# Longformer attention and MLP mixer on one core: global rows by one-hot matmuls, an MLP head tile by tile, transposes moved over the period edge, one normalisation per query tile, first casts on ScalarE

## The chip, the cores and the metric

The kernel runs on one core of one Trainium2 chip. The metric is the device time of one execution in microseconds (us). A timed comparison runs both kernels in the same rounds on the same chip.

Names: PE is TensorE (PEld its weight loads), DVE VectorE, ACT ScalarE, POOL GpSimd, SP SyncE.

## The reference

Eight batches, eight heads, 576 positions, head size 64. Attention has a band of 32 positions to each side and eight global positions, which see all and are seen by all. The result is laid out as 576 x 512 and goes through a mixer: an MLP over tokens with a residual, and an MLP over channels with a residual.

```python
scores = scale * np.matmul(q, k.transpose(0, 1, 3, 2))
mask = np.abs(pos[:, None] - pos[None, :]) <= 32
mask = mask | is_global[:, None] | is_global[None, :]
attn = softmax(np.where(mask, scores, -1e9))          # shortened
x = (attn @ v).transpose(0, 2, 1, 3).reshape(B, S, H * D)
h = np.maximum(xt @ w_tok1, 0.0) @ w_tok2             # xt: x with tokens last
u = x + h.transpose(0, 2, 1)
out = u + np.maximum(u @ w_ch1, 0.0) @ w_ch2
```

## The kernel before

The work is arranged in periods. In period b the channel MLP of batch b (`dense`: tiles `b1p_*` of M4, then `op_*` of M5) is merged on PE with the attention and the token MLP of batch b+1 (`sparse`). Batch 0 has no partner for its attention, so a preamble of 58 us comes first, in which PE mostly waits. The parts that the change and the argument touch:

```python
def gather_t(t):                     # global rows of four batches, fetched by indirect DMA on POOL
    pg = psv([P, 2, P], F16, name=f"pg_{t}")
    for ti in range(2):
        nc.vector.tensor_copy(out=g16[ti][t], in_=g32[ti][t])
        nc.tensor.transpose(out=pg[:, ti, :], in_=g16[ti][t], identity=ident)
    ...
def norm(b, tau, hf, sh, ps):        # twice per query tile, once per half of the heads
    nc.vector.reciprocal(out=rr[r], in_=pq[r, :, D])
    nc.vector.tensor_tensor(out=x16s[b % 2][...], in0=pq[r, :, 0:D], in1=rr[r]..., op=ALU.mult)

def M1(b, ch):                       # token MLP, first layer
    ...
    nc.scalar.activation(out=a1, in_=ps, func=AF.Relu)        # 128 x 1024

def M2(b, part):                     # second layer and residual, two token tiles at a time
    ...
    nc.vector.tensor_add(out=s["u16"][:, 2*part : 2*part+2], in0=x16[:, 2*part : 2*part+2], in1=ps)

def M3(b, part):                     # transpose of u: by PE for batch 0, by DMA for the others
    if part < 2 and b == 0:
        ...
    elif part < 2:
        for i in range(2):
            tau = 2 * part + i
            nc.sync.dma_start_transpose(out=s["uT"][:, :, P*tau : P*tau+P], in_=s["u16"][:, tau, :])

def sparse(b):                       # (weight, work); merge() spreads it over the dense work of b-1
    u = [(8.0 if b == 1 else 0.5, lambda: globals_(b))]
    u += [t(0), t(1), sa(0), sb(0), t(2), sm(0), sa(1), sb(1), t(3), ...]
    ...
    u += [(1.3, lambda: (M2(b, 0), M3(b, 0))), (1.3, lambda: (M2(b, 1), M3(b, 1)))]
    u += [(6.0, lambda: (M2(b, 2), M3(b, 2) if b % 2 else None))]

def cast0(p):                        # batch 0: f32 to f16, q on ACT, k on DVE
    cast_qk(0, slice(2*p, 2*p + 2), (nc.scalar.copy, nc.vector.tensor_copy))

cast0(0); T(0, 0); TE(0, 0); masks_a(); cast0(1); gather_t(0); globals_(0)
T(0, 1); TE(0, 1); S_(0, 0, 0); masks_b(); cast0(2); ...
```

`T` is ten PE transposes of a pair of heads, `TE` their four copies out of PSUM by DVE. `S_` is scores and exp, `SM` the two masked products per pair of heads on DVE (`e_all`). POOL clears `e_all` with one large memset early in the preamble. In the tile names `pv` is the attention output, `a1p` and `hp` are the two layers of the token MLP, `u` is x plus their result (`ul` its last rows), `uT` the transpose of `u`, `b1p` and `op` are the two layers of the channel MLP and `osb` the output. The first channel matmul of batch b+1, `b1p_0`, needs the four DMA transposes `uT` of that batch.

The softmax here doesn't subtract the row's maximum and nothing guards it: scores larger than these inputs give would overflow.

## Time and profile before

| | before |
|---|---|
| median of 4 runs, in the rounds shared with the changed kernel | 376.06 us (374.57 to 377.19) |
| span of the profiled run, mean clock | 375.8 us, 0.979 |
| first PV matmul (end of the wait for attention of batch 0) | 40.06 us |
| end of the token MLP's first layer (`a1p`) | 49.58 us |
| first channel matmul `b1p_0` of batch 0 | 58.45 us |

From the page of the kernel before: span, busy time by engine, two rows of the 40 slices (each digit the busy share of a slice in tenths; PEclk the granted clock), and the chain of work that ended last, by engine.

```profile
span 375.8 us, 6776 instructions
...
PE 319.2 (85%) x2713; PEld 168.2 (45%) x2713; DVE 202.4 (54%) x507; ACT 136.6 (36%) x269; POOL 117.3 (31%) x167
...
PE   0145868988699998999699989997999989997994
...
PEclk9999989999899999999899999999899999999998
...
PE 71%; DVE 12%; ACT 6%; DMA 6%; SPq 3%; issue 2%; DVEq 0%; ACTq 0%
```

PE is busy for 85% of the span and carries 71% of the last chain. The first six digits of its row are where it is not yet busy.

The stage table of the kernel before, cut at the three moments of the small table. Columns: the stretch, its length, busy time of each engine with the number of instructions, granted clock, DMA share, GB/s.

```profile
...
core 0: us, PE busy (x) PEld busy (x) DVE busy (x) ACT busy (x) POOL busy (x), PEclk, DMA share, GB/s
0.00:40.06 40.06, 12.38 (x115) 7.50 (x116) 29.93 (x87) 12.71 (x27) 28.00 (x61) 1.00 0.91 194
40.06:49.58 9.52, 8.99 (x92) 5.86 (x92) 5.82 (x20) 0.00 (x1) 7.07 (x9) 1.00 0.96 192
49.58:58.45 8.87, 4.82 (x26) 2.24 (x26) 3.87 (x5) 1.02 (x1) 7.72 (x11) 0.81 1.05 175
58.45:375.80 317.35, 293.05 (x2480) 152.61 (x2479) 162.80 (x396) 122.90 (x241) 74.51 (x89) 0.98 0.68 78
```

In the first 40.06 us DVE is busy for 29.93, PE for 12.38: the preamble is bound by DVE and what it waits for. In the last row PE is busy for 293.05 of 317.35 us. The 1.00 of the first stretch says nothing: the clock record of this profile begins only at 46.09 us, and what lies before a record is printed as 1.00.

The chain of waits of the kernel before around 17 us (start, length, what), and the timeline of POOL at that time (start, length, engine, line, operation, tiles):

```profile
...
17.21 2.26 DVE g_k_170 L324
```

```profile
...
17.12 2.26 POOL L254 MEMSET e_all<- 128x2560 f16 x1
```

The cast of the gathered rows is a 128x128 piece of work; it took 2.26 us exactly while the POOL memset of 2.26 us ran.

The waits of PE in the kernel before, for the first channel matmul of each period: who waited, at which line, for whom, us in total, times, longest.

```profile
...
PE b1p_0_2209 L571 <- DMA uT_2150<-u_3_2136: 2.8, 1, 2.8
PE b1p_0_3240 L571 <- DMA uT_3181<-u_5_3167: 2.7, 1, 2.7
PE b1p_0_1178 L571 <- DMA uT_1111<-u_1_1104: 2.6, 1, 2.6
PE b1p_0_4240 L571 <- DMA uT_4197<-u_7_4183: 2.5, 1, 2.5
PE b1p_0_2760 L571 <- DMA uT_2695<-u_4_2678: 1.4, 1, 1.4
```

At these edges PE waits for the DMA transposes of the next batch, or, into batch 2, for DVE (the last `osb`). With the two that are cut (1.3 us into batch 6 and 1.2 into batch 2) it is 14.5 us in all.

### The profile page before, as it was taken

The page shows a single profiled execution, that of the slowest core. Times are in us where ns is not written, and L with a number is a line of the kernel's source. Part 1 is how long each engine was busy: PE and PEld are TensorE (multiplying, and loading weights), DVE is VectorE, ACT ScalarE, POOL GpSimd, SP SyncE. Part 2 cuts the span into 40 slices and gives each one's busy share as a digit, 9 for nine tenths or more (in the row PEclk, how much of TensorE's full clock was granted, in tenths as well). Part 3 has the DMA queues.
Part 4 walks back from the last instruction along what each step waited for, and adds up shares of the span by engine and source line. Part 5 has one row for each costly group of instructions (what it writes and reads, how often), then busy time and mean ns, then how long its engine had stood idle before and what let it go on. Part 6 is the DMA issues. An engine that isn't in the chain of part 4 may idle for free.

```text
span 375.8 us, 6776 instructions
## 1 busy us (share of the span) xinstructions
PE 319.2 (85%) x2713; PEld 168.2 (45%) x2713; DVE 202.4 (54%) x507; ACT 136.6 (36%) x269; POOL 117.3 (31%) x167
## 2 busy tenths in 40 slices
PE   0145868988699998999699989997999989997994
PEld 0022524454255644464346535453547444553541
DVE  3888644875347562765246554764366546753021
ACT  2036014921078014911196007801492119411610
POOL 7992589962008300750035300930000000000000
PEclk9999989999899999999899999999899999999998
DMA  5959999998509953996339841994200140015012
GB/s 150 252 94 240 261 164 119 130 141 74 127 2 120 81 103 84 67 126 81 105 20 118 103 96 53 113 99 90 72 2 29 57 113 0 2 58 127 2 56 84
DMA packets 127487, 35.81 MB, mean 95 GB/s; under 512 B 114656, under 2 KB 122720, under 8 KB 127456
## 3 DMA queue, kind: packets, MB, share of 16 engines
q0 software_dynamic: 88768, 14.65, 51.4%
q1 hardware_dynamic: 38400, 20.72, 20.5%
q8 instruction: 21, 0.34, 0.4%
q14 instruction: 10, 0.08, 0.1%
q10 hardware_dynamic: 288, 0.01, 0.0%
HBM read 36.12 MB, written 9.44 MB: 121 GB/s over the span
## 4 chain that ended last, share of the span: by engine, by line
PE 71%; DVE 12%; ACT 6%; DMA 6%; SPq 3%; issue 2%; DVEq 0%; ACTq 0%
SPq L560 3%; DMA lq<-in_q_dram 1%; DVE e_all L434 1%; ACT e_all L415 1%; ACT e_all L424 1%; DMA uT_1111<-u_1_1104 1%; ACT e_all L422 1%; ACT e_all L423 1%; PE op_4_4431 L597 1%; PE op_3_3737 L597 1%; PE op_4_1695 L597 1%; PE op_3_2706 L597 1%; PE op_3_4415 L597 1%; PE op_2_4399 L597 1%; PE op_1_4383 L597 1%
## 5 line engine op out<-in xcount | busy, mean ns | idle before, releaser
L571 PEld LDWEIGHTS <-wc_180 128*128 128x128 f16 x384 | 32.8, 99 | 55.1 <-issue 22.4
L434 DVE TENSOR_TENSOR e_all<-e_all,bandm 128x1040 f16<-128x1040 f16 x64 | 41.9, 696 | 1.2
L340 POOL DMA_DIRECT2D qn_83<-in_q_dram x15 | 13.5, 898 | 46.1 <-PE pT_3_1297 L370 23.4
L484 PEld LDWEIGHTS <-e_all 128*128 128x128 f16 x320 | 25.0, 100 | 5.8 <-issue 2.3
L340 POOL DMA_DIRECT2D qn_84<-in_q_dram x15 | 13.2, 879 | 40.8 <-PE pT_3_2873 L370 20.1
L489 PEld LDWEIGHTS <-e_all 128*128 128x128 f16 x256 | 19.0, 101 | 1.3
L345 POOL DMA_DIRECT2D vsh_87<-in_v_dram x15 | 12.8, 895 | 16.6 <-PE pv_1_1_1516 L489 2.5
L345 POOL DMA_DIRECT2D vsh_88<-in_v_dram x15 | 12.6, 839 | 16.0 <-PE pv_1_1_982 L489 1.5
L340 POOL DMA_DIRECT2D kn_85<-in_k_dram x15 | 13.6, 907 | 0.0
L532 PEld LDWEIGHTS <-w_179 128*128 128x128 f16 x80 | 7.9, 100 | 12.2 <-issue 4.3
L340 POOL DMA_DIRECT2D kn_86<-in_k_dram x15 | 13.3, 888 | 0.0
L428 DVE TENSOR_TENSOR eg<-e_all,bandm 128x160 f16<-128x160 f16 x32 | 7.5, 236 | 10.6 <-ACT e_all L424 10.6
L370 PEld LDWEIGHTS <-qn_83 128*128 128x128 f16 x80 | 7.1, 119 | 13.6 <-ACT qn_83 L352 9.2
L404 PEld LDWEIGHTS <-kT_125 64*128 64x128 f16 x160 | 6.2, 101 | 13.8 <-issue 13.0
L584 PEld LDWEIGHTS <-wc_180 128*128 128x128 f16 x192 | 10.9, 98 | 0.6
L601 DVE TENSOR_TENSOR osb_0_4380<-u_7_4183,op_0_4367 128x512 f32<-128x512 f16 x1 | 0.7, 686 | 17.7 <-PE op_0_4367 L597 17.7
L404 PEld LDWEIGHTS <-kT_126 64*128 64x128 f16 x160 | 5.2, 94 | 10.1 <-issue 3.8
L370 PEld LDWEIGHTS <-kn_85 128*128 128x128 f16 x80 | 6.8, 120 | 4.8 <-DVE kn_85 L352 4.4
L370 PE MATMUL pT_0_215<-ident,qn_83 128*128 128x128 f16 x5 | 0.7, 309 | 8.7 <-ACT qn_83 L352 8.7
L512 PEld LDWEIGHTS <-w_177 128*128 128x128 f16 x64 | 5.6, 99 | 5.0
L370 PEld LDWEIGHTS <-qn_84 128*128 128x128 f16 x80 | 5.7, 98 | 3.5
L597 PEld LDWEIGHTS <-b_7_4239 128*128 128x128 f16 x48 | 4.7, 98 | 5.4
(1308 smaller groups left out, 845.4 us busy)
## 6 DMA issues: line engine op xcount, KB each, us to landing
lv<-in_v_dram SPq DMA_DIRECT2D x6, 256.0 KB, 8.4
wc_180<-in_moe_w_ch_dram POOLq DMA_DIRECT2D x3, 512.0 KB, 7.1
wc_181<-in_moe_w_ch_dram POOLq DMA_DIRECT2D x3, 512.0 KB, 7.7
qn_83<-in_q_dram POOLq DMA_DIRECT2D x12, 128.0 KB, 4.3
kn_85<-in_k_dram POOLq DMA_DIRECT2D x12, 128.0 KB, 4.4
qn_84<-in_q_dram POOLq DMA_DIRECT2D x12, 128.0 KB, 4.2
kn_86<-in_k_dram POOLq DMA_DIRECT2D x12, 128.0 KB, 4.3
vsh_87<-in_v_dram POOLq DMA_DIRECT2D x9, 128.0 KB, 4.2
```

What stands on the lines that cost most here:

```text
L340: nc.gpsimd.dma_start(out=dst[b % 2][0:n, t], in_=ten[b, :, P * t : P * t + n, :].rearrange("h p d -> p h d"))
L345: nc.gpsimd.dma_start(out=vsh[b % 2][r0:r1, c, :, 0:D], in_=v[b, :, j0 : j0 + (r1 - r0), :].rearrange("h p d -> p h d"),)
L370: nc.tensor.transpose(out=pT[:, ti, P * t : P * t + P], in_=n[b % 2][:, t, 2 * p : 2 * p + 2, :], identity=ident)
L404: nc.tensor.matmul(ps[:, par, off : off + n], lhsT=kT[r, P * c : P * c + P], rhs=qf[r, lo : lo + n], start=True, stop=True,)
L434: nc.vector.tensor_mul(out=eh, in0=eh, in1=bandm)
L484: nc.tensor.matmul(o, lhsT=e_all[:, h, tau, EW - P - sh : EW - sh], rhs=vsh[b % 2][:, tau, h, :], start=False, stop=last and tau == NT - 1,)
L489: nc.tensor.matmul(o, lhsT=e_all[:, h, tau + 1, 0:P], rhs=vsh[b % 2][:, tau + 1, h, :], start=False, stop=last)
L532: nc.tensor.matmul(ps[:, i, :], lhsT=w2[:, ch, P * tau - sh : P * tau - sh + P], rhs=s["a1"][:, ch, :], start=(ch == 0), stop=(ch == 1),)
L560: nc.sync.dma_start_transpose(out=s["uT"][:, :, P * tau : P * tau + P], in_=s["u16"][:, tau, :])
L571: nc.tensor.matmul(ps, lhsT=wc1[:, cc, P * j : P * j + P], rhs=s["uT"][:, cc, :], start=(cc == 0), stop=(cc == 3))
L584: nc.tensor.matmul(ps[:, i, :], lhsT=wc1[:, cc, P * j : P * j + P], rhs=s["uTl"][:, cc, :], start=(cc == 0), stop=(cc == 3),)
L597: nc.tensor.matmul(ps, lhsT=w, rhs=wc2[:, j, :], start=(j == 0), stop=(j == NJ - 1))
```

## The change

The intent: shorten the DVE work ahead of the first PV, shorten the head of the first batch's MLP, and fill the waits at the period edges. Its core, cut:

```diff
+    def G0(p):      # batch 0: global rows as one-hot matmuls on PE (N = 8), no gather
+        for ti, n in enumerate((qn, kn)):
+            for t in range(NT):
+                nc.tensor.matmul(pg[:, p, ti, :], lhsT=n[0][:, t, 2*p : 2*p+2, :], rhs=ohq[:, t, :], ...)
...
     def cast0(p):
-        cast_qk(0, ..., (nc.scalar.copy, nc.vector.tensor_copy))
+        cast_qk(0, ..., (nc.scalar.copy, nc.scalar.copy))
...   # masks_b: nine narrow scalar_tensor_tensor -> four wide products; mf: DVE -> POOL
-        nc.vector.tensor_scalar(out=mf, in0=it_f, ...)
+        nc.gpsimd.tensor_scalar(out=mf, in0=it_f, ...)
...   # the large memset of e_all moves behind masks_c; gather(0) moves to the end of the preamble
-    nc.gpsimd.memset(e_all[:, :, :, 0:64], 0.0)
+    masks_c()
+    nc.gpsimd.memset(e_all[:, :, :, 0:64], 0.0)
...   # PV: one two-bank PSUM tile (psV bufs 2 -> 1), one reciprocal and one product per query tile
-        for hf in range(2):
-            norm(b, tau, hf, sh, pss_[hf])
+        nc.vector.reciprocal(out=rr[r], in_=pq[r, :, :, D])
+        nc.vector.tensor_tensor(out=x16s[b % 2][r, tau, :]..., in0=pq[r, :, :, 0:D], in1=rr[r]..., op=ALU.mult)
...   # head of batch 0: relu in two halves, residual and transposes tile by tile, copies on ACT
+        if b == 0:
+            nc.scalar.activation(out=a1[:, 0], in_=ps[:, 0], func=AF.Relu)
+            nc.vector.tensor_scalar(out=a1[:, 1], in0=ps[:, 1], scalar1=0.0, scalar2=None, op0=ALU.max)
-    for part in range(3):
-        M2(0, part)
-        if part < 2:
-            M3(0, part)
+    M23_first(0); M23_first(1); M3_first(0); M23_first(2); M3_first(1)
+    M23_first(3); M3_first(2); M3_first(3); M2(0, 2)
...   # edges: globals and the first two transposes of batch b+1 go to the end of sparse(b)
-        u = [(8.0 if b == 1 else 0.5, lambda: globals_(b))]
-        u += [t(0), t(1), sa(0), ...]
+        if b < 3:
+            u += [(8.0 if b == 1 else 0.5, lambda: globals_(b)), t(0), t(1)]
...
-        u += [(6.0, lambda: (M2(b, 2), M3(b, 2) if b % 2 else None))]
+        u += [(3.0, lambda: (M2(b, 2), M3(b, 2) if b % 2 else None))]
+        if 3 <= b + 1 < B:
+            n = b + 1
+            u += [(0.5, lambda: globals_(n)), (1.5, lambda: (T(n, 0), TE(n, 0))), (0.5, lambda: (T(n, 1), TE(n, 1)))]
+        else:
+            u += [(2.0, lambda: None)]
```

The loads of batch b+2 are split and issued from inside `sparse(b)` (q and k after the last transposes that read the old tiles, v after the last PV). In the preamble `load_wt()` and `pads(0)` also change place, and the copy `it_f` that `mf` reads goes to POOL with it.

## The prediction

> **What bounds it now.** The page gives PE 85% of the span, DVE 54%; the chain that ended last is 71% PE. From about 58 us on, matmuls run almost back to back, and what is lost sits at the edges between batches. Until then (a first-batch preamble of 58.45 us, to the first channel matmul b1p_0) PE is busy for only 26 us; the chain of waits there runs mostly through DVE: g_k cast 2.26 us (held up while POOL's 2.26 us memset runs), masks, four 1.5 us transpose evictions, k casts squeezed between them.
>
> **Preamble, three parts (chain and timelines of before).**
> 1. To the first PV matmul, 40.1 us. Removed from DVE: 8 k casts (about 4.5 us with their slow ones), gather casts and copies (about 3.5 us), nine narrow mask products (3.1 us to four wider, est. 1.7), mf (1.1 us, goes to POOL). POOL loses four gathers (5.2 us). Added: 40 matmuls with N=8, est. 1 us per pair, in PE idle time. All casts on ACT delay the first transposes by about 0.5 us. Following DVE through the new order, with the two score PSUM buffers, I get the first PV at 33.5 to 35.5, so 5.5 us saved.
> 2. PV and first token matmul: 40.1 to 49.6. Normalisation per tile instead of per half: two times 0.2+0.43 becomes est. 0.95 us, alternating PSUM: about 1 us saved.
> 3. MLP head: 49.6 to 58.45. Relu 1.03 us split over two engines, adds 1.22 us halved (0.69) and overlapped, uT copies to ACT: est. 6.4 instead of 8.9 us.  2.4 us saved.
>
> Sum 9 us, all on the critical path.
>
> **Period edges.** Waits list: b1p_0 waits for the DMA transposes 2.6, 1.2, 2.8, 1.4, 2.7, 1.3, 2.5 us. Landing follows the first hp group by 7.7 us: add 1, four serial issues of 1.3 on the SP queue, 2.5 landing. After three of these waits the next 20 to 30 matmuls run slow (b1p_0 1.50 to 1.87 us instead of 0.86), costing about 1.8 us each[...]. The change puts 1.1 us of transposes and 0.3 us of scores into five of seven edges (into batches 2 to 6): 1.5 us each at the two long ones, 0.55 at the three short (there hp_1 moves later), and the two slow-clock episodes should mostly go (3 us). Edge 0 to 1: same slot, but hp_1 comes 1.3 us earlier: 1.3 saved. Edge 6 to 7: nothing fills it, hp_1 comes later: 1.3 lost, perhaps 1.7 more by clock. PV now has one two-bank buffer: norm 1.0 us against 1.29 us of interposed matmuls, hidden mostly; M4 stage fuller for ACT (14 of 17 us busy): 1 us lost. Net 5 us.
>
> **Prediction.** 376.5 − 9 − 5 = 362.5 us; 8 in 10: 357 to 368. Faster by over 2%: 0.93; within 2%: 0.06; slower: 0.01.
>
> **What would show it.** First b1p_0 near 49.5; first PV near 34.5; b1p_0 waits of about 1 us or less into batches 2 to 6, longer than 3 into 7; no long stall of pv on norm.
>
> **What would make it wrong.** POOL's memsets and casts blocking DVE f16 products; weight loads, now issued earlier, delaying q/k landings; ACT saturating in M4; PE colder in the sparser head; single PV buffer stalls.

The 1 us per pair for the one-hot matmuls names no source and is the author's estimate; the trace of after has the ten of the second pair within 0.45 us (13.85 to 14.30).

## More of the kernel before

A difference of one or two microseconds between two medians can be clock alone.

## The result

The changed kernel took 361.89 us in the median of 4 runs (361.25 to 363.89), against 376.06 us. The ratio is 0.9635, with a 95% interval from 0.9583 to 0.9687. Ratios here and below are the mean time of one kernel's runs over that of the other's of the same rounds, so not quite the ratio of the medians quoted.

The page of the changed kernel, the same lines as before:

```profile
span 359.5 us, 6784 instructions
...
PE 316.5 (88%) x2753; PEld 167.6 (47%) x2753; DVE 186.2 (52%) x420; ACT 140.8 (39%) x281; POOL 121.8 (34%) x171
...
PE   0466789896999999898999989898999999996994
...
PEclk9999999999899999999999999999999999998999
...
PE 71%; DVE 13%; ACT 6%; DMA 4%; issue 2%; SPq 2%; another core or an unknown queue 0%; DVEq 0%
```

The stage table of the changed kernel, cut at its first PV, the end of `a1p` and its first `b1p_0`; columns as in the table of before:

```profile
...
0.00:32.55 32.55, 12.70 (x154) 8.94 (x155) 22.05 (x74) 15.75 (x35) 27.73 (x53) 1.00 1.02 218
32.55:41.37 8.82, 8.39 (x92) 5.80 (x92) 4.45 (x10) 0.00 (x0) 8.61 (x16) 1.00 1.22 212
41.37:48.30 6.93, 4.25 (x28) 1.78 (x28) 4.27 (x8) 2.94 (x5) 6.62 (x11) 1.00 1.16 190
48.30:359.50 311.20, 291.21 (x2482) 151.10 (x2481) 155.47 (x328) 122.07 (x241) 78.89 (x94) 0.99 0.72 82
```

The three preamble stretches are 7.5, 0.7 and 1.9 us shorter (40.06 to 32.55, 9.52 to 8.82, 8.87 to 6.93), and the periods 6.15 us (317.35 to 311.20). In the first stretch DVE lost 7.9 us of work (29.93 to 22.05) and PV came 7.5 us earlier, so the stretch shrank nearly one for one with DVE. These differences come to 16.3 us, and the medians differ by 14.2: the profiled execution of before took 377.74 us, more than any of its four timed runs, and that of after was the fastest of its four.

The waits of PE at the edges of the changed kernel:

```profile
...
PE b1p_0_4137 L594 <- DMA uT_4094<-u_7_4071: 3.2, 1, 3.2
PE b1p_0_1195 L594 <- DMA uT_1152<-u_1_1131: 2.6, 1, 2.6
PE b1p_0_2751 L594 <- DMA uT_2667<-u_4_2638: 1.2, 1, 1.2
```

They belong to batches 7, 1 and 4. Two more are cut, 0.7 us into batch 5 and 0.6 into batch 3; into 2 and 6 there is no wait left. Taking the time from each `b1p_0` to the next, the periods changed as follows (positive: shorter).

| period, from the `b1p_0` of batch | 0 | 1 | 2 | 3 | 4 | 5 | 6 | 7, to the end |
|---|---|---|---|---|---|---|---|---|
| before, us | 42.54 | 43.13 | 38.10 | 43.41 | 37.92 | 43.33 | 37.78 | 31.14 |
| after, us | 41.18 | 43.06 | 37.05 | 41.68 | 37.15 | 40.41 | 37.94 | 32.73 |
| shorter by | 1.36 | 0.07 | 1.05 | 1.73 | 0.77 | 2.92 | -0.16 | -1.59 |

The last value is a clock drop. The timeline of PE in the changed kernel at the edge into batch 7 (the second number of a row is the time that a group of matmuls took, x4 the number in it, the bracket the idle time before):

```profile
...
326.77 1.02 PE L594 MATMUL b1p_0_4137<-uT_4094,wc_181 128*128 128x512 f16 x4 [3.20 <-DMA uT_4094<-u_7_4071]
327.63 1.65 PE L594 MATMUL b1p_1_4143<-uT_4094,wc_181 128*128 128x512 f16 x4
329.07 1.91 PE L594 MATMUL b1p_2_4149<-uT_4094,wc_181 128*128 128x512 f16 x4
330.78 1.29 PE L594 MATMUL b1p_3_4155<-uT_4094,wc_181 128*128 128x512 f16 x4
```

Four 128x512 matmuls took 1.03 us in each of the eight rows that follow (`b1p_4` to `b1p_11`, cut). Here three groups took 1.65, 1.91 and 1.29 us after an idle of 3.20 us.

### The profile page after: what moved, and what is told of

It is laid out like the page before. It is cut to its first block, busy times and chain, and to the rows that moved or that the text cites. A ratio compares the mean times of both kernels' runs of the same rounds, so it can differ in the third digit from the quotient of the medians.

```text
span 359.5 us, 6784 instructions
## 1 busy us (share of the span) xinstructions
PE 316.5 (88%) x2753; PEld 167.6 (47%) x2753; DVE 186.2 (52%) x420; ACT 140.8 (39%) x281; POOL 121.8 (34%) x171
## 4 chain that ended last, share of the span: by engine, by line
PE 71%; DVE 13%; ACT 6%; DMA 4%; issue 2%; SPq 2%; another core or an unknown queue 0%; DVEq 0%
DVE e_all L452 3%; ACT e_all L433 2%; DMA lq<-in_q_dram 1%; SPq L583 1%; ACT e_all L442 1%; ACT e_all L441 1%; DMA uT_2667<-u_4_2638 1%; PE op_4_4328 L620 1%; PE op_3_2168 L620 1%; PE op_3_1163 L620 1%; PE op_3_4312 L620 1%; PE op_2_4296 L620 1%; PE op_1_4280 L620 1%; PE op_0_4264 L620 1%; PE op_2_4081 L620 1%
## 5 line engine op out<-in xcount | busy, mean ns | idle before, releaser
L594 PEld LDWEIGHTS <-wc_181 128*128 128x128 f16 x384 | 32.8, 99 | 47.3 <-issue 17.2
L505 PEld LDWEIGHTS <-e_all 128*128 128x128 f16 x256 | 19.1, 101 | 1.3
L344 POOL DMA_DIRECT2D vsh_88<-in_v_dram x15 | 12.7, 879 | 13.9 <-PE pv_0_1964 L505 1.7
L388 PEld LDWEIGHTS <-qn_83 128*128 128x128 f16 x80 | 6.3, 110 | 11.6 <-ACT qn_83 L351 8.5
L607 PEld LDWEIGHTS <-wc_181 128*128 128x128 f16 x192 | 11.1, 98 | 0.8
L548 PEld LDWEIGHTS <-w_180 128*128 128x128 f16 x72 | 7.0, 98 | 8.4
L524 PEld LDWEIGHTS <-w_178 128*128 128x128 f16 x64 | 5.6, 99 | 4.9 <-issue 0.2
L388 PEld LDWEIGHTS <-qn_84 128*128 128x128 f16 x80 | 5.7, 98 | 3.8 <-issue 0.7
L620 PEld LDWEIGHTS <-b_7_4136 128*128 128x128 f16 x48 | 4.7, 98 | 5.4
L620 PEld LDWEIGHTS <-b_6_3726 128*128 128x128 f16 x48 | 4.6, 98 | 5.2
```

What stands on the lines that cost most here:

```text
L344: nc.gpsimd.dma_start(out=vsh[b % 2][r0:r1, c, :, 0:D], in_=v[b, :, j0 : j0 + (r1 - r0), :].rearrange("h p d -> p h d"),)
L388: nc.tensor.transpose(out=pT[:, ti, P * t : P * t + P], in_=n[b % 2][:, t, 2 * p : 2 * p + 2, :], identity=ident)
L505: nc.tensor.matmul(o, lhsT=e_all[:, h, tau + 1, 0:P], rhs=vsh[b % 2][:, tau + 1, h, :], start=False, stop=last)
L594: nc.tensor.matmul(ps, lhsT=wc1[:, cc, P * j : P * j + P], rhs=s["uT"][:, cc, :], start=(cc == 0), stop=(cc == 3))
L607: nc.tensor.matmul(ps[:, i, :], lhsT=wc1[:, cc, P * j : P * j + P], rhs=s["uTl"][:, cc, :], start=(cc == 0), stop=(cc == 3),)
L620: nc.tensor.matmul(ps, lhsT=w, rhs=wc2[:, j, :], start=(j == 0), stop=(j == NJ - 1))
```

## The experiments

Twelve kernels ran, all timed in three rounds, all correct, each with one profile. "Before" means the kernel before in the same rounds; its medians were 375.59, 375.56, 377.34 and 375.56 us in the four groups of rounds.

### edges_only: the kernel before with only the new `sparse` schedule and its loads

```diff
-    def sparse(b):  # of before
+    def sparse(b):  # of after, load_qk16 and load_v16 in it
```

> The kernel before with the new sparse schedule and its loads alone (transposes of batches 3 to 7 moved over the period edge, the loads with them); preamble, normalisation and PV buffers as before. Theory: filling the waits at the edges is worth what the two traces differ by after the first channel matmul, 16.3 - 10.0 = 6.3 us, whatever the preamble does: about 370 us (369 to 371), the five filled edges wait about 1.1 us or less, the edge into batch 7 waits over 3 us. Rival: the edge gain depends on the other parts (merged normalisation frees the vector engine there): then 373 or more, and new waits on the vector engine or on PV buffers show in the periods.

Measured: 368.80 us (368.19 to 370.78), ratio 0.9821 [0.9767, 0.9875], so faster, but not clear of 2%. From the first `b1p_0` to the end it took 310.5 us, against 317.35 in before and 311.20 in after. The whole gain of the periods comes from the schedule and is there without any preamble change. The wait into batch 7 was 3.20 us here too, but this time no slow stretch followed: the next 25 matmuls took 5.60 us.

This run also cleared up the head. It has the old head, but reached it with another history of the clock. The timelines of PE in the head (here the second number is the time of a group, x8 or x4 the matmuls in it), before first, then edges_only:

```profile
...
52.99 1.04 PE L550 MATMUL pu_0_611<-ident,u_0_602 128*128 128x128 f16 x8 [1.32 <-DVE u_0_602 L537]
53.82 1.91 PE L532 MATMUL hp_1_621<-a_0_600,w_179 128*128 128x512 f16 x4
```

```profile
...
52.12 0.62 PE L552 MATMUL pu<-ident,u 128*128 128x128 f16 x8 [1.31 <-DVE u L539]
52.58 1.03 PE L534 MATMUL hp<-a,w 128*128 128x512 f16 x4
```

The same eight transposes took 1.04 us in before and 0.62 here, the same four `hp_1` matmuls 1.91 and 1.03. The head of the kernel before had lost about 1.2 us to the clock (8.87 us from `a1p` to `b1p_0`, 7.66 here), behind two idle times of PE of 1.11 and 1.32 us.

### head_only: the kernel before with only the tile-by-tile head

```diff
-        nc.scalar.activation(out=a1, in_=ps, func=AF.Relu)
+        ...   # relu in two halves for batch 0
-    for part in range(3): M2(0, part); M3(0, part)
+    M23_first(0); M23_first(1); M3_first(0); ...
```

> The kernel before with the tile-by-tile MLP head of batch 0 alone (with the split relu and the transposed copies on the scalar engine). Theory: the head from the end of the first token matmul to the first channel matmul goes from 8.9 to about 7.1 us, as in the changed kernel, and the time to about 374.3 us. Rival: the head gains only beside the rest of the change (a warmer TensorE, a freer vector engine): then under 0.7 us of it shows, the time stays at 375.5 or more.

Measured: 375.63 us (372.43 to 376.70), ratio 0.9974 [0.9905, 1.0043]; by time alone inconclusive. In the profile the head takes 5.92 us, at a clock of 1.00. Against the 7.66 us of edges_only, also at 1.00, the tile-by-tile head is worth 1.7 us; against the profiled run of before it shows 2.9. The rest of that profile, after `b1p_0`, was 1.2 us longer than in before (318.56 and 317.35 us), and it hides the gain: after `b1p_0`, and before the drop at the very end, the clock was halved for 13.7 us in this profile and for 10.2 us in that of before. In after the head takes 6.93 us and not 5.92: there the casts and transposes of the late gather of batches 1 to 3 are issued on DVE and PE ahead of `b1p_0`. gather_clear, below, has the head of after without this late gather, and there it takes 5.91 us.

### gather_back: the changed kernel with the indirect gather for batch 0 again

```diff
+    gather(0)                       # early, as in before
-    G0(0); G0(1); G0(2); G0(3)
+    gather_t(0); globals_(0)
```

> The changed kernel with batch 0's global rows fetched by the indirect gather again (issued early on POOL, cast, transposed, copied), all else as changed; no one-hot matmuls. Theory: what the preamble gained is the shorter chain through the vector engine (k casts moved to the scalar engine, wider mask products, no cast held by a memset), not the one-hot rows: first PV matmul at 33 to 34.5 us instead of 32.6, time 362 to 364 us. Rival (the title of the change): the gather itself was the cost, so first PV goes back to 36 us or later and the time to 366 or more.

Measured: 368.81 us (367.23 to 371.16, 6 runs), ratio 0.9806 [0.9763, 0.9850], not clear of 2%. First PV at 39.58 us, 7.0 later than in after. By its limits (36 us or later, 366 us or more) the rival came true, but its reason did not, as gather_clear shows. The timeline of DVE in this run, the last pair of masked products (x2, one record), and of POOL at that time:

```profile
...
32.42 5.68 DVE L453 TENSOR_TENSOR e_all<-e_all,bandm 128x1040 f16<-128x1040 f16 x2
```

```profile
...
33.27 1.88 POOL L352 CAST qn<-lq 128x2048 f16<-128x2048 f32 x1
...
35.66 1.88 POOL L352 CAST kn<-lk 128x2048 f16<-128x2048 f32 x1
```

The same two products take 1.31 us, and 5.68 us when POOL casts q and k of batch 1 beside them. With the gather issued early, POOL gets to its casts for batch 1 at 33.27 us, while DVE, which is late, still has its last products to do; in after the casts start at 36.71 us, when the products have been done for 6 us. Why DVE is held is not shown. What the traces show is which DVE work took longer beside POOL work: products of two SBUF inputs (5.68 us against 1.31 here) and casts from SBUF (2.33 us beside the memset in before, 0.62 in memset_only, below). DVE copies from PSUM of 128x512 took 0.68 to 0.69 us with or without POOL work beside them.

### gather_clear: gather_back, with POOL's casts for batch 1 kept away

```diff
         load_wc1(h0)
+    gather(1)                       # in the slot where after issues gather(0): POOL is busy longer
     SM(0, 3)
...
-            gather(1)
```

> As gather_back (batch 0's global rows by the indirect gather), but the second gather of POOL is issued where the changed kernel issues its first, so that POOL's casts of batch 1 start some 5 us later and no longer run beside the last mask product of batch 0, which took 5.7 us instead of 1.3 in gather_back. Theory: of the 7 us that gather_back lost, 4.4 were that collision, and about 3 us are the gather's own cost on the vector engine: first PV matmul at 35 to 36 us (after: 32.6, gather_back: 39.6), time 364 to 365.5 us. Rival: the loss is the gather's own latency whatever POOL does: first PV stays at 38 us or later, time at 367.5 or more.

Measured: 364.12 us (363.76 to 367.31, 5 runs), ratio 0.9688 [0.9651, 0.9724]; first PV at 34.85 us. The last pair of products in the timeline of DVE:

```profile
...
32.47 1.31 DVE L453 TENSOR_TENSOR e_all<-e_all,bandm 128x1040 f16<-128x1040 f16 x2
```

So the 7.0 us of gather_back are two things: the gather itself, with what its early issue delays on POOL, 2.3 us (34.85 against 32.55), and an accident of order on POOL, 4.7 us (39.58 against 34.85). The one-hot matmuls are worth the first number, give or take: in seven profiles with the preamble of after the first PV lay between 31.91 and 32.60 us.

### memset_only: the kernel before with one memset moved behind the v casts

```diff
-    nc.gpsimd.memset(e_all[:, :, :, 0:64], 0.0)
     ...
     castv(0)
+    nc.gpsimd.memset(e_all[:, :, :, 0:64], 0.0)
```

> The kernel before with one POOL memset (the 128x2560 pads of e_all, 2.26 us) moved from before the v casts to after them, nothing else. Theory: the vector engine's cast of the gathered k rows (2.3 us) was only held by this memset, so it falls to about 0.3 us and the first PV matmul comes about 2 us earlier (38 us), time about 374.2. Rival: the hold only moves to another vector instruction that then runs beside the memset (mask products or k casts grow by 1 us or more), first PV stays within 0.7 us of 40.1, time 375.5 or more.

Measured: 376.57 us (376.40 to 376.72), ratio 1.0017 [0.9973, 1.0061]: nothing gained; first PV at 39.43 us, 0.6 earlier, as the rival said. The timeline of DVE in this run:

```profile
...
17.11 0.62 DVE L323 CAST g_k<-g_k 128x128 f16<-128x128 f32 x1
...
23.43 1.93 DVE L351 CAST kn<-lk 128x512 f16<-128x512 f32 x1
```

The cast that took 2.33 us in the timeline of before takes 0.62 us, but a k cast that took 0.53 us there takes 1.93 us, because the memset now runs from 22.86 to 25.1 us beside it. Here the hold on DVE moved with the POOL work. In after the memset runs from 19.10 to 21.32 us, when DVE copies from PSUM or waits for PE, and it holds nothing.

### casts_back: the changed kernel with batch 0's k casts on DVE again

```diff
-        cast_qk(0, ..., (nc.scalar.copy, nc.scalar.copy))
+        cast_qk(0, ..., (nc.scalar.copy, nc.vector.tensor_copy))   # and between the pairs, as in before (so the q casts on ACT come later too)
```

> The changed kernel with batch 0's k casts back on the vector engine, each just before its pair's transposes as before (q casts stay on the scalar engine); one-hot rows and all else as changed. Theory: three of the four k casts (about 0.65 us with the last rows) then stand in the vector engine's chain, and each also puts a TensorE transpose after it into that chain: first PV matmul at 34.6 to 36.5 us instead of 32.6 (31.9 to 32.6 in runs with that preamble), time 363.5 to 366. Rival: the vector engine idles 2.0 us in the chain anyway (20.1 to 22.2, waiting for the fourth pair's transposes), so the casts fit in there: first PV under 33.3, time as changed.

Measured: 365.28 us (363.52 to 366.15), ratio 0.9728 [0.9698, 0.9758]; first PV at 37.78 us, 5.2 later than in after, and later than expected. The timeline of DVE, two of the three 128x512 k casts that came back between the pairs (the last of them is cut, and a fourth, the first pair's, runs at 8.80 us):

```profile
...
17.15 0.83 DVE L351 CAST kn<-lk 128x512 f16<-128x512 f32 x1
...
20.30 1.52 DVE L351 CAST kn<-lk 128x512 f16<-128x512 f32 x1
```

Beside `mf`, the memset and the v casts of POOL they took 0.83, 1.52 and 0.75 us, where an undisturbed one took 0.44 us in before; the small casts of the last rows add 0.21, 0.62 and 0.62 us. Together that is 4.6 us more of DVE time. DVE also waited for PE between the copies of the pairs, 0.68, 0.38 and 2.43 us, against 2.02 us in one place in after; how the two share the 5.2 us isn't separated. Taken back alone, the move of the k casts to ACT (5.2 us) is worth more than the move from the gather to matmuls (2.3). The parts can't be added up, because each part taken back also shifts where POOL's work falls.

### old_norm: the changed kernel with the normalisation per half

```diff
-    psV = ... bufs=1
+    psV = ... bufs=2
-        nc.vector.reciprocal(out=rr[r], in_=pq[r, :, :, D])
+        for hf in range(2): norm(b, tau, hf, sh, pss_[hf])
```

> The changed kernel with the normalisation per half and two one-bank PV buffers, as before. Theory: the merged normalisation is worth the 0.7 us by which the stage from first PV to the end of the first token matmul got shorter, and nothing later (vector engine is not on the path there): that stage back at 9.3 to 9.6 us instead of 8.8, periods unchanged, time 362.3 to 363. Rival A: it also paid in the periods: time 364 or more. Rival B: the single two-bank buffer costs in the periods as much as the merge gains: time 361.5 or less.

Measured: 360.11 us (357.13 to 362.25), ratio 0.9581 [0.9508, 0.9653]. The PV stage took 9.5 us instead of 8.8, as the theory said. That this is the merge is not shown, because the stage begins with slow matmuls. The clock record of these profiles begins, at full speed, at 46.09 us in before, 37.76 in after, 38.03 here, and what PE does ahead of that moment takes longer, so the moment is read here as a rise of the clock. The timeline of PE in after, two matmuls of the same shape before that rise (1.04 us) and two after it (0.59):

```profile
...
35.15 1.04 PE L524 MATMUL a1p_551<-x_0_192,w_178 128*128 128x512 f16 x2
...
38.68 0.59 PE L524 MATMUL a1p_551<-x_0_192,w_178 128*128 128x512 f16 x2
```

From the first PV to the rise it is 5.2 us in after and 6.1 here. In the nine profiles with the merge the stage took 8.2 to 9.0 us, in the five without it 8.9 to 9.5. Less half of the time before the rise it is 6.2 to 6.3 us with the merge and 6.5 to 6.7 without, so the merge is worth some 0.3 us, an estimate from these traces; the rest of the 0.7 us is when the clock rose. All period starts agree with those of after within 0.36 us, so the merge is worth nothing in the periods. That the total is lower than after's is clock: its wait into batch 7 was 3.20 us too, without a slow stretch behind it, and its last stretch took 31.15 instead of 32.73 us.

### relu_tiles: the changed kernel with the two relu halves in two SBUF tiles

```diff
+            a1x = mb.tile([P, DM], F16, tag="a1x", bufs=1, name="a1x")
-            nc.vector.tensor_scalar(out=a1[:, 1], in0=ps[:, 1], scalar1=0.0, scalar2=None, op0=ALU.max)
+            nc.vector.tensor_scalar(out=a1x, in0=ps[:, 1], scalar1=0.0, scalar2=None, op0=ALU.max)
```

> The changed kernel with the two halves of batch 0's relu in two tiles. In the changed kernel the vector engine's half starts at 42.02, just after the scalar engine's half ended (41.39 + 0.60). Theory: they are ordered only because both write one tile; in two tiles both start together, and the head shortens by about 0.65 us (first MLP matmul pair done 0.65 us earlier; from end of token matmul to first channel matmul 6.3 instead of 6.95). Rival: the vector engine waits for something else (PSUM reads of one tile), nothing changes. Time: 361.3 or so, inside the noise either way.

Measured: 361.28 us (359.38 to 362.69), ratio 0.9610 [0.9556, 0.9663]; the head 6.95 us, unchanged. The DVE half still starts (41.65 us) when the ACT half ends (41.02 + 0.60). The shared output tile isn't what orders them. The shared PSUM input tile remained as the suspect, and best_a tests it.

### warm_edges and warm_wide: dummy PE work in the waits into batches 1 and 7

```diff
         merge(sparse(b + 1) if b + 1 < B else [], dense(b))
+        if b in (0, 6):
+            for i in range(40):   # warm_edges: 40 transposes of 128 columns
+                nc.tensor.transpose(out=pw[:, i % 8, :], in_=ident, identity=ident)
```
```diff
+            for i in range(16):   # warm_wide instead: 16 matmuls of 512 columns
+                nc.tensor.matmul(pw[:, i % 2, :], lhsT=ident, rhs=wc2[:, i % NJ, :], start=True, stop=True)
```

> The changed kernel with 40 dummy transposes (about 2.2 us of TensorE work, results unread) in the two waits that nothing fills: into batch 1 and into batch 7. Theory: the slow matmuls after these waits (1.87 instead of 0.86 us for a group of four; 5.15 instead of 3.46 us for the first four groups of batch 7) come from the idle TensorE clock, so they go, the landings of the transposes do not move, the mean granted clock rises to 0.99 or more in every run and the time falls by 2 to 3 us to about 359.5. Rival: the slow stretches have another cause (DMA or SBUF traffic at the edge): they stay, time 361.5 or more.

> As warm_edges, but the filler is 16 matmuls of 512 columns (about 3.5 us at full clock) instead of 40 transposes of 128. In warm_edges the serial issue of the four DMA transposes took 6.6 us (into batch 1) instead of 5.2, so the landings moved out and the waits stayed 2.9 and 2.0 us. Theory: idle time is what drops the clock, and the slower issue came with the dense train of small instructions: with the wide filler the issues take 5.2 us again, the waits shrink to about 1 us or less, the first groups of batch 1 and batch 7 run at full speed (about 0.86 us a group) and the time falls to about 359.5. Rival: any TensorE work at that point delays the landings by as much as it fills: waits stay over 2 us, time 361.5 or more.

warm_edges: 362.32 us (361.26 to 363.59), ratio 0.9630 [0.9591, 0.9669]. It settled nothing about the clock, because the waits stayed: 2.88 us into batch 1 and 2.04 into 7, with slow stretches behind both. The four DMA transposes, issued one after the other on SP at that time, took longer. The timeline of SP in warm_edges:

```profile
...
82.56 6.56 SPq L583 DMA_TRANSPOSE uT<-u  x4
```

In after the same issue took 5.22 us, in warm_wide 5.23. Why the train of narrow transposes lengthened it stays open.

warm_wide: 359.54 us (358.80 to 359.96), ratio 0.9546 [0.9499, 0.9594]. The waits fell to 0.33 and 0 us and no slow stretch followed. Stage tables of the first microseconds behind the edge into batch 7, after first, then warm_wide; the third value from the right is the granted clock:

```profile
...
326.77:332.00 5.23, 5.23 (x17) 2.08 (x18) 0.00 (x0) 1.79 (x3) 0.00 (x0) 0.67 0.27 76
```

```profile
...
325.96:331.00 5.04, 5.04 (x25) 2.28 (x24) 0.00 (x0) 2.87 (x5) 0.00 (x0) 1.00 0.28 80
```

0.67 became 1.00. (Behind the edge into batch 1 it was 0.50 in after and 1.00 here.) So the slow stretches here are a clock drop that came with PE's idle time, 2.6 and 3.20 us in after, and with 16 matmuls of 512 columns in the wait, whose results nobody reads, it did not come. By medians, each from its own rounds and chip, that is 2.4 us against after (361.89 to 359.54), for work that computes nothing.

### best_a and best_c: useful work in the waits

best_a puts the two halves of batch 0's first-layer result into two PSUM tiles, moves the gather's transposes later, lets the first two transposes of batch 2 cross the edge into batch 1, and places batch 7's token MLP earlier. best_c also starts batch 1's attention earlier in its period and leaves more for the edge.

```diff
-            s["a1p"] = pss([P, 2, 512], name=f"a1p_{b}")
+            if b == 0:
+                s["a1p"] = [psm([P, 512], name=f"a1p_0_{tt}") for tt in range(2)]
...
-        if 3 <= b + 1 < B:
+        if 2 <= b + 1 < B:
...
-            u += [(2.0, lambda: None)]
+            u += [(8.0, lambda: None)]
...   # best_c, on top of best_a
-        u += [(8.0, lambda: None), (0.5, lambda: (gather_t(0), globals_(b))), t(0), t(1)]
+        u += [(3.0, lambda: None), (0.5, lambda: (gather_t(0), globals_(b))), t(0), t(1)]
-            u += [(0.5, lambda: globals_(n)), ...]
+            u += [(5.5 if n == 2 else 0.5, lambda: globals_(n)), ...]
```

> The changed kernel with four additions: (1) the two relu halves of batch 0 read two one-bank PSUM tiles (in relu_tiles, two SBUF tiles alone did not separate them); (2) the gather transposes for batches 1 to 3 come after the fifth channel matmul instead of before the first, those for batches 4 to 7 in the middle of a period; (3) the transposes of batch 2 also go over the edge; (4) batch 7's token MLP comes earlier before the end of the period, so that 7.8 us of matmuls follow hp_0 instead of 5.2. Theory: head 5.3 us instead of 6.95 (0.65 by the relu, 1.0 by the gather), edge into batch 1: wait 2.4 instead of 3.5 with 1.4 us of work done in it, edge into batch 7: wait under 0.7 us instead of 3.2 and no slow stretch: about 354.5 us (353 to 357). Rival for (1): the pair stays ordered, head 5.9. Rival for (4): scalar or vector engine can't follow in the tighter period and new waits there take back over 2 us: 358 or more.

> As best_a, and the period of batch 0 starts batch 1's attention two channel matmuls earlier and ends with more dense work after hp_0 (7.9 us instead of 5.3), so that the edge into batch 1 is filled too. Theory: wait there under 0.7 us, no slow stretch: another 2 to 3.5 us, 351 to 353.5 us. Rival: batch 1's casts or the second channel weights aren't there yet so early, and the wait moves into the period: 354 or more.

best_a: 359.03 us (356.10 to 360.07), ratio 0.9538 [0.9488, 0.9589]. Its head is 5.28 us. The timelines of the two relu halves in after (DVE, then ACT):

```profile
...
42.02 0.69 DVE L530 TENSOR_SCALAR a_0_620<-a1p_551 128x512 f16<-128x512 f32 x1 [1.31 <-ACT a_0_620 L529]
```

```profile
...
41.39 0.60 ACT L529 ACTIVATE a_0_620<-a1p_551 128x512 f16<-128x512 f32 x1 [11.61 <-PE a1p_551 L524]
```

and in best_a (DVE, then ACT):

```profile
...
40.85 0.69 DVE L539 TENSOR_SCALAR a1x<-a1p 128x512 f16<-128x512 f32 x1 [0.68 <-PE a1p L532]
```

```profile
...
40.63 0.60 ACT L538 ACTIVATE a<-a1p 128x512 f16<-128x512 f32 x1 [10.88 <-PE a1p L532]
```

In after the DVE half began at 42.02 us, after ACT's ended, and the pair took 1.3 us where the undivided relu of before took 1.03. In best_a they overlap by 0.38 us. The only relevant difference from relu_tiles is the second PSUM tile, so the order came from sharing one PSUM tile in the program, not from the engines. The median stayed above the expected 353 to 357 us, and above the 358 of the rival, although the profiled run, at a clock of 0.999, was 356.10; two other runs had 0.989 and 0.990. The wait into batch 7 is gone (0.03 us), but PE now waits 2.33 us inside the period of batch 1 for the DVE casts of the gather for batches 4 to 7, which moved there; best_c has this wait too.

best_c: 355.19 us (354.58 to 355.85), ratio 0.9431 [0.9382, 0.9481], the fastest of all, 6.7 us below after by medians of different rounds. From its page:

```profile
span 353.0 us, 6781 instructions
...
PEclk9999999999999999999999999999999999999999
```

The clock stayed at nine tenths or more, the top digit, in all 40 slices, and its mean was 0.998. Waits of PE at the edges are left only into batches 3, 4 and 5 (0.62, 1.54 and 0.74 us). It came 1.7 us above the upper end that had been expected of it, in the range of its rival. Nearly all of its gain over after stands in the head (1.7 us) and in periods 6 and 7 (66.1 us against 70.7), where batch 7's token MLP comes earlier; periods 0 and 1, which the filled edge into batch 1 was to shorten, take 83.7 us against 84.2.

## Why the prediction was right

The total was predicted as 362.5 us and measured as 361.89, inside the range, and the direction was right. Term by term, in the profiled runs:

| term | predicted | measured | what the runs showed |
|---|---|---|---|
| first PV | 5.5 us (at 33.5 to 35.5) | 7.5 us (32.55) | undersized |
| PV stage | 1 us | 0.7 us | oversized: some 0.3 us by the merge, the rest by when the clock rose (old_norm) |
| MLP head | 2.4 us | 1.9 us | two errors that nearly cancel |
| period 0 | 1.3 us | 1.36 us | |
| periods 1 to 5 | 6.65 us (3 + 1.65 + 3 clock - 1) | 6.54 us | edges_only |
| edge 6 to 7 | -1.3 us | -0.16 us | |
| clock behind it | -1.7 us | -1.59 us | warm_wide |

The terms add up to 13.9 us as predicted and 16.3 as measured, so the close agreement of the totals is in part luck: the first PV was undersized by 2 us, and the profiled pair differs by 2.1 us more than the medians do.

1. The mis-sized step is "Following DVE through the new order, with the two score PSUM buffers, I get the first PV at 33.5 to 35.5". DVE's saving was nearly all on the path: 7.9 us of its busy time gone, 7.5 us gained. The gather alone is worth 2.3 us (gather_clear), and the k casts on ACT up to 5.2 us (casts_back), since back on DVE they are held beside POOL's work (0.83, 1.52 and 0.75 us against 0.44). A share of this the prediction had read right: the 2.26 us cast beside the memset. What it left out is that moving the memset alone only moves the hold (memset_only), and that the new order keeps POOL's casts for batch 1 clear of the last products, which costs 4.7 us where it goes wrong (gather_back). The wider mask products took 1.7 us (15.18 to 16.91) where the narrow ones took 3.2 (22.35 to 25.56), as estimated; they and the move of `mf` were not taken back alone.
2. "mf (1.1 us, goes to POOL)" counts DVE time that goes away, rightly. On POOL it is not the same work at the same price: the last instruction took 3.78 us there instead of 0.61 on DVE. It cost nothing, since `mf` was ready at 19.1 us and the product that needs it ran at 30.66 us.
3. The PV stage: the estimate of 0.95 us for the merged normalisation was close (0.21 + 0.69 us in the trace), but the stage did not shorten by what DVE saved: of the 0.7 us some 0.3 are the merge.
4. The head: "Relu 1.03 us split over two engines" did not split; the halves ran one after the other (1.3 us) because they read one PSUM tile (from two, in best_a, they overlap by 0.38 us), and the late gather added about 1 us ahead of `b1p_0`. On the other side, 1.2 us of the old head was a clock drop which the prediction had read as work, and the new head has none. Written as a sum: 1.2 (clock) + 1.7 (tile by tile) - 1.0 (gather) = 1.9 us.
5. The edges: the waits of 2.84 and 2.66 us fell to 0.6 and 0.7 us, and with them both clock drops behind them went, as predicted. Period by period the agreement is less good than in the sum (1.05, 1.73, 0.77 and 2.92 us for periods 2 to 5). The loss at the edge into batch 7 was foreseen, 3.2 us of wait and a clock drop; the period before it was 0.5 us shorter otherwise, so only 0.16 of the 1.3 us was lost. Profiled runs of other kernels with the same wait of 3.20 us there have no clock drop (edges_only, old_norm, casts_back), so the 1.59 us are luck, good or bad, as the next paragraphs show.
6. Of the dangers named, POOL blocking DVE's f16 products is real (5.68 us for 1.31 in gather_back), but the change's order avoids it. ACT saturation, late q and k, and stalls of the single PV buffer do not show: old_norm, with two buffers, has the same period starts.

On the clock the records of the profiles show more. In those of before and after every stretch between two changes, up to the drop at the end, is a whole number of times 3.41 us: full clock for 2, 13, 23, 23 and 31 times 3.41 us in before and for 15, 69 and 8 times in after, and half clock for 3.41 us at each drop between. In gather_back and gather_clear the half clock lasted longer, all the 5.20 us behind the edge into batch 7. This grid of 3.41 us, with slots of that length, does not lie at one place of the kernel: at the edge into batch 7 a slot ends 1.12 us after the first `b1p_0` in after (327.89 and 326.77 us) and 1.61 us ahead of it in before (343.05 and 344.66). Stage tables cut at each run's grid, at the edge into batch 7, after first, then edges_only; the second number is the length, the third the time that PE was busy, the third from the right the clock:

```profile
...
324.48:327.89 3.41, 1.12 (x6) 0.56 (x7) 0.00 (x0) 0.00 (x0) 0.00 (x0) 1.00 0.49 95
327.89:331.31 3.42, 3.42 (x10) 1.22 (x9) 0.00 (x0) 1.48 (x3) 0.00 (x0) 0.50 0.21 78
```

```profile
...
330.96:334.37 3.41, 1.47 (x7) 0.49 (x5) 1.12 (x2) 0.00 (x0) 0.00 (x0) 1.00 0.61 155
334.37:337.79 3.42, 2.16 (x10) 1.00 (x11) 0.00 (x0) 0.84 (x2) 0.00 (x0) 1.00 0.57 152
```

The idle time is 3.20 us in both. In after most of it falls into one slot, in which PE is busy for a third, and the next slot gets half the clock. In edges_only it is spread over two slots, and nothing drops. The same edge in all runs that idle there, with the granted clock in the 5.2 us behind the edge:

| run | idle, us | clock behind |
|---|---|---|
| head_only | 2.52 | 0.67 |
| gather_back | 3.20 | 0.50 |
| after, relu_tiles | 3.20 | 0.67 |
| gather_clear | 3.20 | 0.50 |
| warm_edges | 2.04 | 0.67 |
| edges_only | 3.20 | 1.00 |
| memset_only | 2.52 | 1.00 |
| casts_back | 3.20 | 1.00 |
| old_norm | 3.20 | 1.00 |
| before | 2.52 | 1.00 |

The same wait of 3.20 us was followed by a drop in four profiles and by none in three, and 2.04 us were enough in warm_edges. How idle a slot was sorts the cases in the two profiles whose slots were counted: of the 182 full-clock slots of before and after, from the start of each record to the drop at its end, PE was busy for 0.11 to 0.33 in the six that a drop followed, and for 0.53 or more in all others. What lies between these two profiles do not show; the 1.47 of 3.41 us in edges_only, 0.43, brought no drop. So in these profiles it mattered how much idle time fell into one slot, and as the grid lies differently against the kernel from run to run, what follows a wait of 2.5 to 3.2 us is, as far as these runs show, a matter of luck.

## What to carry to other kernels

Where a stage is bound by DVE, look first at its SBUF-to-SBUF casts and products that run beside POOL work: moving casts to ACT, or POOL's casts and memsets to a time when DVE only reads PSUM, gained more here than the bare durations say (5.2 us for k casts of 0.44 us each, casts_back; 4.7 us between gather_back and gather_clear). Waits of PE of 2 to 3 us at the edges of a pipeline can cost more than themselves, because the clock may drop behind them (1.59 us behind the 3.20 us in after); filling them with work that has to be done anyway paid in edges_only, by letting the next batch's first transposes cross the edge, and in best_a and best_c, by placing the last batch's token MLP earlier. And when one tile is read by two engines in halves, check in the timeline that they overlap: a second PSUM tile was what it took here (no overlap in relu_tiles, 0.38 us in best_a).
